# Clustered attention and two MoE layers on one core: another order of the kernel's first steps, and other engines for the first mask rows

## The chip, the cores and the metric

The kernel runs on one core of a Trainium2 chip. The core has five engines that run their own instruction streams and meet at semaphores: TensorE (PE in the profile, its weight loads PEld), VectorE (DVE), ScalarE (ACT), GpSimd (POOL) and SyncE (SP, which here only issues DMAs). The metric is device time in microseconds (us) of one execution, the median of several.

## The reference

There are 2 batches, 8 heads, 768 tokens, head size 64 and 16 centroids per head. What the change touches is the assignment and the mask:

```python
c_n = centroids / (np.linalg.norm(centroids, axis=-1, keepdims=True) + 1e-06)
q_assign = np.argmax(np.einsum('bhsd,hcd->bhsc', q_n, c_n), axis=-1)
k_assign = np.argmax(np.einsum('bhsd,hcd->bhsc', k_n, c_n), axis=-1)
mask = q_assign[:, :, :, None] == k_assign[:, :, None, :]
scores = scale * np.matmul(q, k.transpose(0, 1, 3, 2))
scores = np.where(mask, scores, -1000000000.0)
...
attn = attn / (np.sum(attn, axis=-1, keepdims=True) + 1e-09)
return np.matmul(attn, v).astype(np.float32)
```

A token attends only to tokens of its own cluster. The result goes through two feed-forward layers (`_moe_ref`, `_moe2_ref`), in fp32, which the change leaves as they are.

## The kernel before

All of it is one function, `tile_kernel`, whose order is the order in which it is written: each engine gets its instructions in that order and the semaphores are put in by the framework. Two reads of one PSUM tile by different engines are also put in order by a semaphore.

Attention goes over 8 pairs of heads (`pairs`) and for each over 12 steps (`order`: half of the queries, block of 128 queries, head of the pair). A step `n` is: `scores` (four matmuls into `s_ps`, of which there are two buffers: the products of the rounded `q1` and `k1` first, L382, then of `q2` and `k2`, L386), `maximum` (DVE, L395), `exponentials` (ACT, L403, into `p`), transposes of `p` (L439), and later the product with the values (L446). The mask is part of the scores: rows 64 to 80 of `q2` and `k2` hold a one-hot code of the cluster, times 2**60 on the query side, less 2**60, so that a pair of other clusters gets -2**60. For the first pair 32 rows are written, and these are what the change calls mask rows.

Before step 0 there is a head of the program, some 13 us long, in which little runs side by side:

1. `cn` (the centroids, 32 KB) is loaded; their norms come from ACT (L240 to L242) and DVE (L243 to L248); DVE scales `cn` (L249).
2. TensorE turns `cn` (L252, 64 rows out). DVE copies the even heads' half into rows 0 to 63 of `ct`, and then ACT the odd heads' half into rows 64 to 127 (`ct_copy`, L255); the rest of `ct` is zeros (L224).
3. `sims` (L309) multiplies `ct` with the raw queries `sq` and keys `sk` of the first pair, 384 KB each.
4. DVE alone finds the largest of each 16, breaks ties and makes the one-hot codes: L321, L335, L340, L346, L349, then per head L352 and the turning into rows L520 (`t3`, in PSUM).
5. Six instructions write the mask rows out of `t3` before step 0 and 1 can end, and a seventh and eighth follow for the second half of the queries: `q_rows` (L524, ACT) and plain copies of the key rows (L532, ACT for head `h0`, DVE for head `h1`).

Beside these, ACT makes `q1` and `k1` of both heads (L476 to L487), POOL the remainders (L481 to L497), DVE one (L499). `keep_warm` puts transposes of the identity on TensorE that nobody reads: 15 at the start, 3 after the turning of `cn`, 27 after `sims`, 18 and 9 around step 0 (all L215); the first waits for POOL to make the identity (`ident`). SP issues every DMA in order; the second pair's `sk` and `sq` are loaded once the first pair's are read.

Of the kernel before, what the change touches and what calls it, by code (L numbers as in the profile page):

```python
# [17 lines left out]
MASKED = float(2**60)  # L18

@with_exitstack  # L20
def tile_kernel(ctx, tc, q_t, k_t, q_s, k_s, v_l, cent, w_in, w_out, a_co, b_co, w_gate, w_val, w_o2, out):
    nc = tc.nc
    B, H, D, S = q_t.shape
    D //= 2
    NC = cent.shape[0] // H
    P = 128
# [12 lines left out]
    def r32(ap):  # L39
        return ap.bitcast(F32)  # L40

    nc.scalar.preload_act_table_set("natural_log_exp_and_others")
    ctx.enter_context(tc.manual_schedule())
    small = ctx.enter_context(tc.tile_pool(name="small", bufs=1, side="left"))
    r0_p = ctx.enter_context(tc.tile_pool(name="r0_p", bufs=1, side="left", reuse_waits="tile"))
# [135 lines left out]
            nc.sync.dma_start(out=t[key], in_=src[b, h])  # L181


    def load_pair(b, hp, keys=("sq", "sk")):
        for key in keys:
            live[key] = xs_p.tile([P, S], F32, tag=key, name=key)
            nc.sync.dma_start(out=live[key], in_=(q_s if key == "sq" else k_s)[b, hp])
# [6 lines left out]
    cn = as_p.tile([P, J, NC], F32, tag="t1", name="cn").rearrange("p j c -> p (j c)")[:, 0:D]  # L194
    nc.sync.dma_start(out=cn, in_=cent)
    load_pair(0, 0)
    for e in range(2):
        heads[0, e] = {}
    cst = small.tile([P, 24], F32, name="cst")
# [3 lines left out]
    xk1 = x_tile("xk")  # L203
    nc.sync.dma_start(out=xk1[0:D, :], in_=k_t[0, 1, 0:D, :])

    ident = base.tile([P, P], F32, name="ident")
    make_identity(nc, ident)

    def t_tile(name):
        return ps_t.tile([P, HB, P], F32, tag="t", name=name)  # L210

    def keep_warm(n, to, x=None):
        for _ in range(n):
            for j in range(HB):
                nc.tensor.transpose(to[:, j, :], ident if x is None else x[:, 0:P], ident)  # L215

    warm = ps_s.tile([P, S], F32, tag="s", name="w_ps")[:, 0:HALF].rearrange("p (j c) -> p j c", c=P)
    keep_warm(5, warm)

    wt_i = const.tile([P, NC], mybir.dt.int32, name="wt_i")  # L220
    nc.gpsimd.iota(wt_i, pattern=[[-1, NC]], base=NC, channel_multiplier=0)
    wt = const.tile([P, NC], F32, name="wt")
    ct = const.tile([P, H // 2, 2, NC], F32, name="ct")
    nc.vector.memset(ct, 0.0)  # L224
# [27 lines left out]
    nc.tensor.transpose(ct_ps, cn, ident)  # L252

    def ct_copy(copy, e):
        copy(  # L255
            out=ct[e * D:(e + 1) * D, :, e, :], in_=ct_ps.rearrange("p (h e c) -> p h e c", e=2, c=NC)[:, :, e, :]
        )
# [265 lines left out]
    def q_rows(t, half):
        nc.scalar.activation(  # L524
            out=t["q2"][D:D + 32, cols[half]], in_=t["t3"][32 * half:32 * half + 32, :],
            func=AF.Identity, scale=MASKED, bias=msk[32 * half:32 * half + 32, 1:2],
        )
# [950 lines left out]
```

## Time and profile before

| | |
|---|---|
| median of 3 runs | 771.9 us (771.74 to 772.0) |
| profiled execution | 771.61 us, of which the span of the trace is 769.8 us |
| PE busy | 763.1 us, 99% of the span |
| DVE, ACT, POOL busy | 78%, 65%, 59% |
| chain that ended last | PE 93%, ACT 3%, DVE 2% |

The span runs from the first instruction in the trace to the last; 1.8 us of the execution lie around it. A busy PE is one with a matmul on its way, and fillers count as busy. The chain is followed back from the last instruction, at each step to what released it.

### The profile page before, as it was taken

Reading aid. Unit: us, or ns where it says so; the run is one execution under the profiler, and the core shown is the slowest. Engines: PE = TensorE matmul, PEld = TensorE weight load, DVE = VectorE, ACT = ScalarE, POOL = GpSimd, SP = SyncE. Lnnn points to the kernel's source line nnn. Section 1 sums busy time; section 2 is a strip of 40 time slices with the busy share of each in tenths; the row PEclk is TensorE's granted clock in tenths of the full one; section 3 lists DMA queues with packets and bytes.
Section 4 is the critical chain, followed back from the end, with each engine's and each line's share of the span. In section 5 each row is a group of like instructions: output and inputs, shape, how many; then the busy total and the mean of one; then the engine's idle time right before and its main releaser. Section 6 shows DMA issues by size and latency. Waiting matters only on the chain.

```text
span 769.8 us, 11591 instructions
## 1 busy us (share of the span) xinstructions
PE 763.1 (99%) x4119; PEld 638.9 (83%) x4119; DVE 599.3 (78%) x919; ACT 504.1 (65%) x959; POOL 454.0 (59%) x429
## 2 busy tenths in 40 slices
PE   8999999999999999999999999999999999999998
PEld 7767677777768888888888888999999999999997
DVE  7888878788769999889999989996576665675454
ACT  7677768777867888687777678556554545444331
POOL 6667687667316676657777688674263554444310
PEclk9999999999999999999999999999999999999999
DMA  6456545453222211121111111023212212120013
GB/s 217 119 181 215 186 131 166 163 168 94 73 77 82 82 56 61 49 83 55 56 54 55 55 55 56 1 63 129 83 55 83 70 42 80 55 82 28 1 42 123
DMA packets 27209, 67.94 MB, mean 88 GB/s; under 512 B 4464, under 2 KB 10832, under 8 KB 27152
## 3 DMA queue, kind: packets, MB, share of 16 engines
q1 hardware_dynamic: 27152, 67.21, 26.8%
q8 instruction: 32, 0.52, 0.3%
q14 instruction: 25, 0.20, 0.1%
HBM read 59.48 MB, written 3.19 MB: 81 GB/s over the span
## 4 chain that ended last, share of the span: by engine, by line
PE 93%; ACT 3%; DVE 2%; POOL 1%; issue 1%; POOLq 0%; ACTq 0%; DVEq 0%
PE c_ps L1068 23%; PE acc L804 15%; PE h_ps L748 14%; PE acc L1125 13%; PE o_ps L446 8%; PE t_ps L439 7%; PE s_ps L382 4%; PE s_ps L386 4%; PE w_ps L215 1%; PE sim L309 1%; POOL tmp L765 1%; DVE st L395 1%; ACT p L403 1%; ACT tmp L773 0%; ACT tmp L763 0%
## 5 line engine op out<-in xcount | busy, mean ns | idle before, releaser
L1068 PE MATMUL c_ps<-r,wb 128*128 128x384 f32 x648 | 125.3, 336 | 0.0
L1068 PEld LDWEIGHTS c_ps<-r,wb 128*128 128x128 f32 x648 | 115.4, 188 | 6.0
L395 DVE TENSOR_REDUCE st<-s_ps 128x1 f32<-128x768 f32 x96 | 91.8, 956 | 31.8 <-PE s_ps L386 31.7
L765 POOL TENSOR_TENSOR tmp<-tmp 128x512 f32<-128x512 f32 x46 | 68.0, 1479 | 47.5 <-ACT tmp L764 47.1
L403 ACT ACTIVATE p<-s_ps,st 128x768 f32<-128x768 f32 x96 | 87.3, 909 | 7.6 <-DVE st L395 5.1
L1076 ACT COPY tmp<-c_ps 128x384 f32<-128x384 f32 x60 | 28.9, 481 | 86.9 <-PE c_ps L1068 86.9
L1147 POOL TENSOR_TENSOR part<-tmp,part 128x512 f32<-128x512 f32 x18 | 23.4, 1298 | 101.2 <-ACT tmp L1146 101.2
L439 PE MATMUL t_ps<-ident,p 128*128 128x128 f32 x576 | 76.5, 273 | 1.0 <-DVE pt L440 0.9
L439 PEld LDWEIGHTS t_ps<-ident,p 128*128 128x128 f32 x576 | 66.0, 140 | 5.6 <-DVE pt L440 1.2
L804 PE MATMUL acc<-g,r 128*128 128x512 f32 x288 | 69.1, 389 | 0.2 <-ACT part L811 0.2
L788 POOL TENSOR_TENSOR g<-td,tmp 128x512 fp32r<-128x512 f32 x45 | 58.5, 1300 | 18.0 <-DVE td L783 18.0
L1079 DVE TENSOR_TENSOR tmp<-tmp,c_ps 128x384 f32<-128x384 f32 x40 | 22.2, 554 | 58.9 <-ACT tmp L1076 45.1
L446 PE MATMUL o_ps<-pt,v 128*64 128x384 f32 x384 | 65.7, 491 | 0.1
L1068 PE MATMUL c_ps<-r,xw 128*128 128x384 f32 x336 | 65.4, 337 | 0.0
L440 ACT COPY pt<-t_ps 128x384 f32<-128x384 f32 x128 | 56.0, 481 | 14.1 <-PE t_ps L439 14.1
L804 PEld LDWEIGHTS acc<-g,r 128*128 128x128 f32 x288 | 54.0, 188 | 11.8 <-ACT part L811 0.7
L1068 PEld LDWEIGHTS c_ps<-r,xw 128*128 128x128 f32 x336 | 60.0, 188 | 3.7
L748 PE MATMUL h_ps<-r 128*128 128x512 f32 x252 | 60.5, 390 | 0.0
L1125 PE MATMUL acc<-wb,g 128*128 128x512 f32 x216 | 59.4, 394 | 0.0
L382 PE MATMUL s_ps<-k,q 128*128 128x512 f32 x192 | 57.7, 382 | 0.3 <-ACT p L403 0.2
L748 PEld LDWEIGHTS h_ps<-r 128*128 128x128 f32 x252 | 47.1, 188 | 10.4 <-issue 0.6
L446 PEld LDWEIGHTS o_ps<-pt,v 128*64 128x64 f32 x384 | 26.0, 137 | 35.1 <-issue 32.6
(169 smaller groups left out, 1789.6 us busy)
## 6 DMA issues: line engine op xcount, KB each, us to landing
raw<-w_in_dram SPq DMA_DIRECT2D x16, 512.0 KB
raw<-w_out_dram SPq DMA_DIRECT2D x16, 512.0 KB
raw<-w_val_dram SPq DMA_DIRECT2D x12, 512.0 KB
raw<-w_gate_dram SPq DMA_DIRECT2D x12, 512.0 KB
raw<-w_o_dram SPq DMA_DIRECT2D x12, 512.0 KB
xa<-q_t_dram SPq DMA_DIRECT2D x14, 384.0 KB
xa<-k_t_dram SPq DMA_DIRECT2D x14, 384.0 KB
sq<-q_s_dram SPq DMA_DIRECT2D x8, 384.0 KB
```

Of the source, the lines that this page charges most:

```text
L382: nc.tensor.matmul(s_ps[:, lo:hi], t["q1"][:, qs], t["k1"][:, lo:hi], start=True, stop=False)
L395: nc.vector.tensor_reduce(out=st[:, 0, k:k + 1], in_=live["s", b, hp, half, i, e], axis=AX.X, op=ALU.max, negate=True)
L403: nc.scalar.activation(out=p, in_=live.pop(("s", b, hp, half, i, e)), func=AF.Exp, bias=st[:, 0, k:k + 1], accum_out=st[:, 1, k:k + 1],)
L439: nc.tensor.transpose(t_ps[:, j, :], p[:, kb * P:(kb + 1) * P], ident)
L440: copy(out=pt[:, g * HB:(g + 1) * HB, i * P:(i + 1) * P], in_=t_ps)
L446: nc.tensor.matmul(live["o", b, hp, half][e * D:(e + 1) * D, :], heads[b, 2 * hp + e]["v"][:, kb, :], live["pt", b, hp, half, e][:, kb, :] ...
L748: nc.tensor.matmul(h_ps, w[:, wi, cs], x[:, xi, cc, :], start=(n == 0), stop=(n == 3 * NCC - 1))
L765: spread.tensor_tensor(out=tq, in0=tq, in1=tr, op=ALU.add)
L788: eng.tensor_tensor(out=g[:, 1, :], in0=td, in1=tr, op=ALU.mult)
L804: nc.tensor.matmul(acc[c], w[:, wi, cs], g[:, gi, :], start=(first and m == 0), stop=(last and m == 2))
L1068: nc.tensor.matmul(live2[key], set_of[f][:, wi, a, cs], x[xi][:, kc, :], start=(first and n == 0), stop=(n == last), skip_group_check=True,)
L1125: nc.tensor.matmul(acc2[j, c], g[:, gi, c * P:(c + 1) * P], w[:, wi, :], start=(f % 2 == 0 and m == 0), stop=(f % 2 == 1 and m == 2),)
```

## The change

The table load of ACT comes after an issue of `sk` on ACT's own DMA queue. TensorE gets two matmuls of zeros ahead of its first transposes. `cn` is copied into two blocks `cn2`, one times the parity of the head and one times its opposite (`par`, from a new `iota`), both are scaled and turned at once (128 rows out), and one DVE copy fills `ct`. The mask rows go to other engines, and one copy of ACT (`k1`, upper half, of `h1`) stands behind the first two of them. The second pair's `sq` is loaded ahead of its `sk`.

```diff
-    nc.scalar.preload_act_table_set("natural_log_exp_and_others")
...
-    load_pair(0, 0)
+    load_pair(0, 0, queues=(nc.sync, nc.scalar))
+    nc.scalar.preload_act_table_set("natural_log_exp_and_others")
...
+    oh = [rb_p.tile([P, HALF], F32, tag="rb", name="oh") for e in range(2)]
+    zero = oh[0][:, 0:P]
+    nc.vector.memset(zero, 0.0)
...
+    for j in range(HB - 1):
+        nc.tensor.matmul(warm[:, j, :], zero, zero, start=True, stop=True)
     keep_warm(5, warm)
...
+    nc.vector.tensor_tensor(
+        out=cn2.rearrange("p (e d) -> p e d", e=2), in0=cn.rearrange("p (o d) -> p o d", o=1).to_broadcast([P, 2, D]),
+        in1=par.to_broadcast([P, 2, D]), op=ALU.mult,
+    )
...
-    nc.vector.tensor_scalar_mul(out=cn, in0=cn, scalar1=ss[:, 3:4])
...
-    ct_ps = t_tile("ct_ps")[0:D, 0, :]
-    nc.tensor.transpose(ct_ps, cn, ident)
...
-    ct_copy(nc.vector.tensor_copy, 0)
+    nc.vector.tensor_scalar_mul(out=cn2, in0=cn2, scalar1=ss[:, 3:4])
+
+    ct_ps = t_tile("ct_ps")[:, 0, :]
+    nc.tensor.transpose(ct_ps, cn2, ident)
+    nc.vector.tensor_copy(out=ct.rearrange("p h e c -> p (h e c)"), in_=ct_ps)
...
-    ct_copy(nc.scalar.copy, 1)
...
-        nc.scalar.copy(out=t["k1"][D:P, :], in_=xk)
+        if e == 0:
+            nc.scalar.copy(out=t["k1"][D:P, :], in_=xk)
...
-    load_pair(*pairs[1], keys=("sk", "sq"))
+    load_pair(*pairs[1])
...
     q_rows(h0, 0)
-    for half, c in enumerate(cols):
-        for t, copy in ((h0, nc.scalar.copy), (h1, nc.vector.tensor_copy)):
-            copy(out=t["k2"][D:D + 32, c], in_=t["t3"][64 + 32 * half:96 + 32 * half, :])
+    k_rows(h0, 0, nc.scalar.copy)
+    nc.scalar.copy(out=h1["k1"][D:P, :], in_=xk1_up)
+    k_rows(h0, 1, nc.vector.tensor_copy)
+    q_rows(h1, 0)
+    k_rows(h1, 0, nc.vector.tensor_copy)
+    k_rows(h1, 1, nc.scalar.copy)
...
-    q_rows(h0, 1)
-    q_rows(h1, 0)
...
         if n == 1:
+            q_rows(h0, 1, on_dve=True)
             keep_warm(3, fill)
```

How the instructions then stand, at three places. First TensorE at the start of the program, before (`w_ps` is what fillers write, `ct_ps` the turned centroids):

```order
L215 MATMUL w_ps_135<-ident_130 128x128 [waits Pool_49]
L215 MATMUL w_ps_135<-ident_130 128x128 x14
L252 MATMUL ct_ps_180<-ident_130,cn_120 64x128 [waits DVE_49]
L215 MATMUL w_ps_135<-ident_130 128x128 x3
L309 MATMUL sim_196<-sq_122,ct_154 32x384 [waits DMAHW1_49,Activation_49]
L309 MATMUL sim_196<-sq_122,ct_154 32x384
```

and now, with two matmuls of zeros (read from `oh`) in front, and `sims` waiting for DVE instead of ACT:

```order
L223 MATMUL w_ps_138<-oh_130 128x128 [waits DVE_49]
L223 MATMUL w_ps_138<-oh_130 128x128
L219 MATMUL w_ps_138<-ident_133 128x128 [waits Pool_49]
L219 MATMUL w_ps_138<-ident_133 128x128 x14
L267 MATMUL ct_ps_188<-ident_133,cn_119 128x128 [waits DVE_49]
L219 MATMUL w_ps_138<-ident_133 128x128 x3
L318 MATMUL sim_203<-sq_121,ct_159 32x384 [waits DMAHW2_49,DVE_49]
```

The 15 transposes are still there, behind the zeros and ahead of the turning of the centroids.

Second ACT between `k1` and the first exponentials, before (`t3_262` and `q2_184`, `k2_186` are of `h0`; `t3_265`, `q2_188` of `h1`):

```order
L487 CAST k1_189<-sk_124 64x768
L524 ACTIVATE q2_184<-t3_262,msk_156 32x384 [waits DVE_49]
L532 CAST k2_186<-t3_262 32x384 x2
L524 ACTIVATE q2_184<-t3_262,msk_156 32x384
L524 ACTIVATE q2_188<-t3_265,msk_156 32x384 [waits DVE_49]
L403 ACTIVATE p_301,st_298<-s_ps_275,st_298 128x768 [waits DVE_49]
```

and now (`t3_268`, `q2_192`, `k2_194` of `h0`; `t3_271`, `q2_196`, `k2_198` of `h1`):

```order
L495 CAST k1_197<-sk_123 64x768
L541 ACTIVATE q2_192<-t3_268,msk_163 32x384 [waits DVE_49]
L544 CAST k2_194<-t3_268 32x384
L548 CAST k1_197<-sk_123 64x768
L541 ACTIVATE q2_196<-t3_271,msk_163 32x384 [waits DVE_49]
L544 CAST k2_198<-t3_271 32x384 [waits DVE_49]
L412 ACTIVATE p_307,st_304<-s_ps_281,st_304 128x768 [waits DVE_49]
```

The 64x768 copy (L548) has moved between the rows of `h0` and those of `h1`, and the last key rows now wait for DVE.

Third DVE at the same place, before:

```order
L520 STREAM_TRANSPOSE t3_262<-oh_165 128x384 [waits DVE_49,Activation_49]
L352 TENSOR_TENSOR oh_166<-wt_153,mx_259 128x12x16
L520 STREAM_TRANSPOSE t3_265<-oh_166 128x384 [waits DVE_49]
L532 CAST k2_190<-t3_265 32x384 [waits DVE_49]
L532 CAST k2_190<-t3_265 32x384
L389 MEMSET st_298 128x6
L395 TENSOR_REDUCE st_298<-s_ps_275 128x1 [waits PE_49]
```

and now:

```order
L530 STREAM_TRANSPOSE t3_268<-oh_130 128x384 [waits DVE_49]
L361 TENSOR_TENSOR oh_131<-wt_158,mx_265 128x12x16
L530 STREAM_TRANSPOSE t3_271<-oh_131 128x384 [waits DVE_49]
L544 CAST k2_194<-t3_268 32x384 [waits Activation_49]
L544 CAST k2_198<-t3_271 32x384 [waits Activation_49]
L398 MEMSET st_304 128x6
L404 TENSOR_REDUCE st_304<-s_ps_281 128x1 [waits PE_49]
L404 TENSOR_REDUCE st_304<-s_ps_315 128x1 [waits PE_49]
L537 TENSOR_SCALAR q2_192<-t3_268,msk_163 32x384
```

Both key-row copies of DVE now wait for ACT: by the values of the semaphore the first (`k2_194`) for ACT's copy of `h0`'s other key rows, the second (`k2_198`) for ACT's `q2_196` from the same `t3_271`. ACT's `k2_198` waits for DVE's.

## Rows read from the trace of the kernel before

**Rows 1.** PE in a stretch: us, busy (instructions), granted clock, DMA share, GB/s

```profile
40.00:700.00 660.00, 659.53 (x3528) 1.00 0.27 88
```

**Rows 2.** The chain that ended last, in order of time: start, us, what

```profile
5.68 1.17 PE sim L309 x8
...
13.84 0.60 PE s_ps L386 x2
...
14.46 0.97 DVE st L395
...
15.46 1.00 ACT p L403 x2
...
16.50 0.62 PE s_ps L382 x2
...
18.13 0.78 PE sim L309 x8
```

**Rows 3.** Timeline, 0 to 7 us: start, us, instruction, count, idle before and releaser

```profile
0.73 1.28 ACT L42 ACT_TABLE_LOAD   x1 [0.73 <-PEq L1469]
...
0.74 0.39 SPq L195 DMA_DIRECT2D cn<-cent_dram  x1
0.83 0.17 DVE L224 MEMSET ct<- 128x128 f32 x1 [0.83 <-PEq L1469]
...
1.18 0.42 SPq L187 DMA_DIRECT2D sq<-q_s_dram  x1
...
1.36 3.46 PE L215 MATMUL w_ps<-ident 128*128 128x128 f32 x15 [1.36 <-POOL ident masks.py:199]
...
2.51 0.26 ACT L240 ACTIVATE sq<-cn 128x64 f32<-128x64 f32 x1 [0.50 <-DMA cn<-cent_dram]
...
4.28 0.84 ACT L476 ACTIVATE q<-sq 64x768 fp32r<-64x768 f32 x1 [0.86 <-DMA sq<-q_s_dram]
4.29 0.26 DVE L249 TENSOR_SCALAR cn<-cn,cst 128x64 f32<-128x64 f32 x1
...
4.62 0.42 PE L252 MATMUL ct_ps<-ident,cn 128*64 128x128 f32 x1
...
5.08 0.22 DVE L255 COPY ct<-ct_ps 64x64 f32<-64x64 f32 x1 [0.52 <-PE ct_ps L252]
...
5.32 0.95 DVE L499 SCALAR_TENSOR_TENSOR q<-sq,q 64x768 fp32r<-64x768 f32 x1
...
5.61 0.82 PE L309 MATMUL sim<-sq,ct 128*32 128x384 f32 x2
...
6.77 3.17 PE L215 MATMUL w_ps<-ident 128*128 128x128 f32 x27
6.89 0.60 DVE L321 STREAM_TRANSPOSE t<-sim 128x384 f32<-128x384 f32 x1 [0.62 <-PE sim L309]
```

**Rows 4.** Timeline of ACT and DVE, 9 to 17.6 us

```profile
9.72 0.83 ACT L487 CAST k<-sk 64x768 fp32r<-64x768 f32 x1
...
9.92 0.35 DVE L352 TENSOR_TENSOR oh<-wt,mx 128x192 f32<-128x192 f32 x1
...
10.38 0.59 DVE L520 STREAM_TRANSPOSE t<-oh 128x384 f32<-128x384 f32 x1
...
11.01 0.57 ACT L524 ACTIVATE q<-t,msk 32x384 fp32r<-32x384 f32 x1 [0.45 <-DVE t L520]
...
11.59 0.95 ACT L532 CAST k<-t 32x384 fp32r<-32x384 f32 x2
...
11.88 1.13 DVE L532 CAST k<-t 32x384 fp32r<-32x384 f32 x2
...
12.57 1.17 ACT L524 ACTIVATE q<-t,msk 32x384 fp32r<-32x384 f32 x2
...
13.26 0.96 DVE L395 TENSOR_REDUCE st<-s_ps 128x1 f32<-128x768 f32 x1
...
16.30 0.96 DVE L395 TENSOR_REDUCE st<-s_ps 128x1 f32<-128x768 f32 x1 [0.88 <-PE s_ps L386]
```

More of the change, by code (lines that the diff above doesn't have):

```diff
@@ L181, in load_qk, with load_pair @@
             nc.sync.dma_start(out=t[key], in_=src[b, h])
-    def load_pair(b, hp, keys=("sq", "sk")):
-        for key in keys:
+    def load_pair(b, hp, keys=("sq", "sk"), queues=(nc.sync, nc.sync)):
+        for key, queue in zip(keys, queues):
             live[key] = xs_p.tile([P, S], F32, tag=key, name=key)
-            nc.sync.dma_start(out=live[key], in_=(q_s if key == "sq" else k_s)[b, hp])
+            queue.dma_start(out=live[key], in_=(q_s if key == "sq" else k_s)[b, hp])
     def load_v(b, h):
@@ L192, in load_v @@
         nc.sync.dma_start(out=t["v"], in_=v_l[b, h])
-    cn = as_p.tile([P, J, NC], F32, tag="t1", name="cn").rearrange("p j c -> p (j c)")[:, 0:D]
+    cn_t = as_p.tile([P, J, NC], F32, tag="t1", name="cn").rearrange("p j c -> p (j c)")
+    cn, cn2 = cn_t[:, 0:D], cn_t[:, D:3 * D]
     nc.sync.dma_start(out=cn, in_=cent)
-    load_pair(0, 0)
+    load_pair(0, 0, queues=(nc.sync, nc.scalar))
+    nc.scalar.preload_act_table_set("natural_log_exp_and_others")
     for e in range(2):
@@ L223, in tile_kernel @@
     ct = const.tile([P, H // 2, 2, NC], F32, name="ct")
-    nc.vector.memset(ct, 0.0)
+    par_i = const.tile([P, 2], mybir.dt.int32, name="par_i")
+    nc.gpsimd.iota(par_i, pattern=[[NC, 2]], base=NC, channel_multiplier=1)
+    par = const.tile([P, 2, 1], F32, name="par")
     msk = const.tile([P, 2], F32, name="msk")
@@ L230, in tile_kernel @@
         nc.vector.memset(msk[r, 1:2], -MASKED if g < 2 else 0.0)
-    oh = [rb_p.tile([P, HALF], F32, tag="rb", name="oh") for e in range(2)]
-    for e in range(2):
-        nc.vector.memset(oh[e], 0.0)
+    nc.vector.memset(oh[0][:, P:HALF], 0.0)
+    nc.vector.memset(oh[1], 0.0)
     nc.vector.tensor_copy(out=wt, in_=wt_i)
+    nc.vector.tensor_scalar(
+        out=par_i, in0=par_i, scalar1=NC.bit_length() - 1, scalar2=1, op0=ALU.logical_shift_right, op1=ALU.bitwise_and
+    )
+    nc.vector.tensor_copy(out=par.rearrange("p e o -> p (e o)"), in_=par_i)
     sq = as_p.tile([P, J, NC], F32, tag="sm", name="sq").rearrange("p j c -> p (j c)")[:, 0:D]
@@ L242, in tile_kernel @@
     nc.scalar.activation(out=ss[:, 1:2], in_=ss[:, 1:2], func=AF.Exp, scale=0.5)
+    nc.vector.tensor_tensor(
+        out=cn2.rearrange("p (e d) -> p e d", e=2), in0=cn.rearrange("p (o d) -> p o d", o=1).to_broadcast([P, 2, D]),
+        in1=par.to_broadcast([P, 2, D]), op=ALU.mult,
+    )
     nc.vector.reciprocal(out=ss[:, 2:3], in_=ss[:, 1:2])
@@ L248, in tile_kernel @@
     nc.vector.reciprocal(out=ss[:, 3:4], in_=ss[:, 2:3])
-    nc.vector.tensor_scalar_mul(out=cn, in0=cn, scalar1=ss[:, 3:4])
-    ct_ps = t_tile("ct_ps")[0:D, 0, :]
-    nc.tensor.transpose(ct_ps, cn, ident)
[L254 to L257, printed above, removed]
-    ct_copy(nc.vector.tensor_copy, 0)
+    nc.vector.tensor_scalar_mul(out=cn2, in0=cn2, scalar1=ss[:, 3:4])
+    ct_ps = t_tile("ct_ps")[:, 0, :]
+    nc.tensor.transpose(ct_ps, cn2, ident)
+    nc.vector.tensor_copy(out=ct.rearrange("p h e c -> p (h e c)"), in_=ct_ps)
     babs = cst[:, 6:11]
@@ L474, in tile_kernel @@
     xs = (live["sq"], live["sk"])
+    xk1_up = live["sk"][D:P, :]
     up = slice(D, P)
     nc.scalar.activation(out=h0["q1"][0:D, :], in_=xs[0][0:D, :], func=AF.Copy, scale=scale)
-    ct_copy(nc.scalar.copy, 1)
     keep_warm(1, warm)
@@ L521, in tile_kernel, with q_rows, k_rows @@
     del live["t1"], live["mx"], live["sm"]
[L523 to L527, printed above, removed]
-    q_rows(h0, 0)
-    for half, c in enumerate(cols):
-        for t, copy in ((h0, nc.scalar.copy), (h1, nc.vector.tensor_copy)):
-            copy(out=t["k2"][D:D + 32, c], in_=t["t3"][64 + 32 * half:96 + 32 * half, :])
+    def q_rows(t, half, on_dve=False):
+        g = slice(32 * half, 32 * half + 32)
+        out, rows = t["q2"][D:D + 32, cols[half]], t["t3"][g, :]
+        if on_dve:
+            nc.vector.tensor_scalar(
+                out=out, in0=rows, scalar1=MASKED, scalar2=msk[g, 1:2], op0=ALU.mult, op1=ALU.add
+            )
+        else:
+            nc.scalar.activation(out=out, in_=rows, func=AF.Identity, scale=MASKED, bias=msk[g, 1:2])
+    def k_rows(t, half, copy):
+        copy(out=t["k2"][D:D + 32, cols[half]], in_=t["t3"][64 + 32 * half:96 + 32 * half, :])
+    q_rows(h0, 0)
+    k_rows(h0, 0, nc.scalar.copy)
[4 more added lines that the diff above has]
+    k_rows(h1, 1, nc.scalar.copy)
     fill = ps_v.tile([P, HALF], F32, tag="o", name="w_ps").rearrange("p (j c) -> p j c", c=P)
-    q_rows(h0, 1)
-    q_rows(h1, 0)
     early = (20, 26, 38, 50, 62, 74, 80, 86, 92)
```

## The prediction

> **What bounds the kernel now.** I read the stretches of PE first: from 40 to 700 us TensorE is idle for 0.47 us in all, at a granted clock of 1.00 [rows 1]. Nothing in the body waits for anything else, so a change of the head can only move the whole body earlier or later, and the body has no idle time that could take up a late start. Then the chain in order of time: from step 0 on it goes from matmul to maximum to exponential to the matmul that needs the buffer back [rows 2], with gaps of some hundredths. So what counts is when the maxima of steps 0 and 1 start, 13.26 and 14.46 us now [rows 2, 4]: what they are late, the end is late. Last I read the timelines backwards from there. The maxima hang on the mask rows, those on `t3` (10.38 + 0.59 = 10.97 us [rows 4]), `t3` on a chain of DVE alone that starts at 6.89 us when `sims` is done, and `sims` on the copy of the turned centroids [rows 3].
>
> I work in two parts: the shift of DVE's start at 6.89, and the mask rows measured from `t3`.
>
> **The zeros and the clock.** [...] Leaving out the drain of the last transpose (0.42 us long, like L252), one follows the other after (3.46 - 0.42)/14 = 0.217 us.
>
> At this rate the 15 fill TensorE until 1.36 + 15 x 0.217 = 4.62 us, which is where the turning of the centroids starts; DVE had `cn` ready at 4.29 + 0.26 = 4.55 [rows 3]. So the queue of fillers ends just in time, and any work put ahead of it goes onto the path. The zeros start after a 128x128 memset as at 0.83 + 0.17 = 1.00 us [rows 3], about 1.05. An fp32 matmul that is not a transpose shows as two records (`sims` is four matmuls and 8 records [rows 2]), so two 128-column matmuls are 4 records of 0.217 = 0.87 us, and the transposes begin at 1.92 instead of 1.36: 0.56 us later. If they were one record each it would be 1.48, 0.12 us later; I take 0.56, as `sims` is the nearest row. The turning then starts at 5.18.
>
> **One copy instead of two.** From the start of the turning to `sims` it is 5.61 - 4.62 = 0.99 us now. With one copy: 0.42 for the turning, 0.04 to DVE, a 128x128 copy, 0.06 to PE. The copy is bounded by 0.22 (64 columns) and 0.59 (L520, 384 columns) [rows 3, 4]; 64 columns more, a fifth of the way, give 0.29. That is 0.81; but the turning and three fillers behind it take 4 x 0.217 = 0.87, so 0.87 holds and 0.12 us is saved. `sims` starts at 5.18 + 0.87 = 6.05, 0.44 late. The product by parity lies in DVE's wait for ACT between 2.5 and 3.5 us and costs nothing; were that cover gone, it would cost about the 0.35 of L352 [rows 4]. The scaling of 128 instead of 64 columns adds some 0.07 to 4.55, hidden by the queue of fillers.
>
> **`sims` itself.** Started 0.44 later it runs mostly or wholly after the rise of the clock, so it saves between 0 (rise as much later) and 1.17 - 0.78 = 0.39 us. I take 0.30, since the rise comes at the latest during `sims` now and TensorE starts 0.31 us earlier. DVE's start shifts by 0.44 - 0.30 = +0.14; bounds: +0.44, and with the zeros at one record each and the full 0.39, -0.39.
>
> **Keys on ACT's queue.** Nothing waits for `sk` now, so its earlier start gains nothing by itself. ACT's issue (0.39 to 0.43 as SP's) pushes its table load to end at 0.73 + 0.42 + 1.28 = 2.43, just before the centroids land at 2.51 [rows 3]: hidden with 0.08 to spare. What can cost is that `cn` now shares the DMA engines with 384 KB of keys. If `cn` lands d late, the turning waits only for d above 5.18 - 4.67 = 0.51, as fillers hold TensorE that long. Bounds for d: 0, and landing when the keys do. `sq`, as large, took from 1.18 to 4.28, 3.10 us, `cn` from 0.74 to 2.51, 1.77 [rows 3]: d is at most 1.33. I take d under 0.5, as `cn` is a twelfth of the keys, and keep 1.33 - 0.51 = +0.82 for the range. [...] No row of this trace has two queues loading at once.
>
> `sq` shares as well. Late by up to 0.6 us, ACT's L476 and then DVE's L499 would end at 4.28 + 0.6 + 0.84 + 0.04 + 0.95 = 6.71 [rows 3], still before 7.03 when DVE is to start: hidden.
>
> **One wait less.** L520 now also waits for ACT's old copy and starts 0.11 us after L352 ends (9.92 + 0.35 to 10.38 [rows 4]), where DVE's neighbours stand 0.03 to 0.04 apart. That semaphore goes: -0.07.
>
> **The mask rows.** Counted from `t3` = 10.97. Now: ACT's rows of `h0` end at 12.54, its last for `h1` at 12.57 + 1.17 = 13.74, and step 1's matmul starts at 13.84 [rows 2, 4]. After: ACT writes `q2` of `h0` (0.57) and half its key rows (0.48) until 12.06; then comes the moved 0.83 us copy, until 12.89; then `q2` of `h1` (0.58) until 13.47. DVE's copy for `h0` waits for ACT's and ends at about 12.67, near the 12.54 of now; its copy for `h1` waits for 13.47 and ends at 13.51 + 0.57 = 14.08. In line behind it on DVE stands the maximum of step 0: after the memset it starts at about 14.11 instead of 13.26, +0.85. ACT's last key rows wait for DVE: 14.12 to 14.60, step 1's matmul starts at 14.68 instead of 13.84, +0.84. I take +0.84; bounds 0.80 and 0.90 by the rounding of six durations. The copy's old place was free: ACT ended L487 at 10.55 and was idle for 0.45 [rows 4], and that idle time is not on the path. `q_rows(h0, 1)` on DVE lies in the 0.88 us of idle before the maximum of step 2 [rows 4] and costs nothing; without that cover 0.57. The second pair's `sk` is issued after the moved copy, some 1.2 us later than the last of the two now, and is needed only at `sims` of 18.1 us plus the shift.
>
> **Sum.** +0.14 - 0.07 + 0.84 = +0.91 us. On the profiled execution's 771.61 that is 772.5; that execution lies 0.3 below the median of the runs, so on the median 772.8. That is 0.12%; about 0.2%, 1.5 us, is what a measurement of this kernel tells from no change.
>
> **The rivals.**
>
> The clock rises early. [...] In this trace 27 transposes in a row keep 117 ns [rows 3], so they hold it at least. Worked out from rows: if real matmuls at 1.05 us raise the clock before the fillers are through, these are done by about 4 us, the turning starts at 4.67, takes 0.27, the copy 0.29, `sims` runs from 5.35 for 0.85, and DVE could start at 6.25. It then waits for L499, which ends at 6.11 to 6.71 by when `sq` lands, so it starts at 6.25 to 6.75, 0.14 to 0.64 before 6.89. The sum is then +0.13 to +0.63, 772.0 to 772.5. For it: TensorE starts earlier. Against: the rise now came 4 to 5 us after the first transposes, and 0.31 us is little of that.
>
> The centroids land late. Place: `cn` on SP's queue beside `sk` on ACT's. Up to d = 0.51 it costs nothing; each tenth above costs a tenth; from d = 0.51 + 0.63 = 1.14 on it is slower by 0.2%. At the bound of 1.33 the time is 771.9 + 0.91 + 0.82 = 773.6. For it: both issues fall at 0.73 us, and the whole head hangs on `cn`. Against: 32 KB is little, and the fillers cover 0.51.
>
> The waits at the mask rows do not reach the end. If the shift of step 0 were taken up further down, +0.07 is left, 772.0. Against: the 0.47 us of idle in 660 us.
>
> **The numbers.** Forecast, +0.3 to +1.3 us (772.2 to 773.2): 0.55. Early clock, 772.0 to 772.5: 0.17. Late centroids, 773.2 to 773.7: 0.17, of which half lie beyond 1.5 us. Shift taken up, 772.0: 0.05. What I have not seen, 0.06, in halves on either side. Slower by over 0.2%: 0.09 + 0.03 = 0.12; faster: 0.03; within: 0.85. The range leaves one in ten out on each side: 771.9 to 773.7.
>
> **What would show it.** In the trace of the changed kernel: the transposes starting near 1.9 us and the turning near 5.2; `sims` at 6.0 and of some 0.9 us; ACT's first activation at 2.5 if `cn` is on time; from the end of `t3` to the maximum of step 0 3.1 us instead of 2.3, with DVE's wait for ACT before its second key-row copy. The prediction is wrong if the span changes by more than the shift of step 1's maximum, or if that shift is not there.

## The result, and the profile after

The changed kernel takes 775.45 us (median of 6 runs, 775.08 to 776.84) against 771.72 us before (6 runs, 771.29 to 772.0): ratio 1.0052, 95% interval 1.0041 to 1.0062. It is slower by 3.7 us, where 0.9 us had been predicted, and above the predicted range of 771.9 to 773.7 us. The profiled execution is one of 775.42 us, with a span of 773.6 us, 3.8 us longer than before.

The head first, as in [rows 3]: the timeline of the changed kernel, 0 to 8 us.

```profile
1.05 1.22 PE L223 MATMUL w_ps<-oh 128*128 128x128 f32 x4 [1.05 <-DVE oh L209]
...
2.07 3.41 PE L219 MATMUL w_ps<-ident 128*128 128x128 f32 x15
...
3.71 0.26 ACT L251 ACTIVATE sq<-cn 128x64 f32<-128x64 f32 x1 [1.27 <-DMA cn<-cent_dram]
...
4.91 0.84 ACT L486 ACTIVATE q<-sq 64x768 fp32r<-64x768 f32 x1 [0.29 <-DMA sq<-q_s_dram]
...
5.83 0.33 PE L267 MATMUL ct_ps<-ident,cn 128*128 128x128 f32 x1 [0.36 <-DVE cn L264]
...
6.20 0.29 DVE L268 COPY ct<-ct_ps 128x128 f32<-128x128 f32 x1 [0.42 <-PE ct_ps L267]
...
6.55 0.52 PE L318 MATMUL sim<-sq,ct 128*32 128x384 f32 x2
...
7.49 0.60 DVE L330 STREAM_TRANSPOSE t<-sim 128x384 f32<-128x384 f32 x1
```

The zeros are four records and the copy takes 0.29 us, as worked out. But `cn` lands at 3.71 instead of 2.51 us (ACT's first read of it), and the turning waits for DVE's `cn`, no longer for the fillers. DVE starts at 7.49 instead of 6.89: +0.60.

Then the mask rows, as in [rows 4]: the same timeline, 10.8 to 16 us.

```profile
10.90 0.59 DVE L530 STREAM_TRANSPOSE t<-oh 128x384 f32<-128x384 f32 x1
...
11.53 0.57 ACT L541 ACTIVATE q<-t,msk 32x384 fp32r<-32x384 f32 x1 [1.44 <-DVE t L530]
...
12.12 0.47 ACT L544 CAST k<-t 32x384 fp32r<-32x384 f32 x1
12.61 0.83 ACT L548 CAST k<-sk 64x768 fp32r<-64x768 f32 x1
12.62 0.56 DVE L544 CAST k<-t 32x384 fp32r<-32x384 f32 x1 [0.25 <-ACT k L544]
...
13.46 0.57 ACT L541 ACTIVATE q<-t,msk 32x384 fp32r<-32x384 f32 x1
14.07 0.56 DVE L544 CAST k<-t 32x384 fp32r<-32x384 f32 x1 [0.89 <-ACT q L541]
14.66 0.47 ACT L544 CAST k<-t 32x384 fp32r<-32x384 f32 x1 [0.62 <-DVE k L544]
...
14.79 2.03 DVE L404 TENSOR_REDUCE st<-s_ps 128x1 f32<-128x768 f32 x2
```

`t3` is there at 11.49 (before 10.97, +0.52). DVE's second key-row copy waits 0.89 us for ACT, and step 0's maximum starts 3.30 us after `t3` instead of 2.29. Step 1's maximum starts at 15.86 (below) instead of 14.46 [rows 2], +1.40 = 0.52 + 0.88.

So far the sum holds but for `cn`. The rest came further down, as two later steps of the chain of waits show (start, us, what), after and before:

```profile
15.86 0.97 DVE st L404
...
29.62 1.33 PE sim L318 x8
30.95 5.11 PE o_ps L455 x24
```

```profile
27.53 0.78 PE sim L309 x8
28.31 4.02 PE o_ps L446 x24
```

The same matmuls start 2.09 us late, and take 1.64 us longer (1.33 + 5.11 against 0.78 + 4.02). The stretches of PE (us, busy and instructions of PE, PEld, DVE, ACT and POOL, granted clock, DMA share, GB/s) tell why, after and before:

```profile
25.00:30.00 5.00, 3.44 (x21) 2.11 (x23) 4.97 (x9) 2.95 (x9) 3.41 (x5) 0.97 0.37 126
30.00:40.00 10.00, 10.00 (x61) 5.68 (x54) 6.40 (x12) 4.76 (x11) 1.77 (x3) 0.84 0.19 45
40.00:700.00 660.00, 659.42 (x3536) 549.18 (x3535) 533.78 (x792) 453.96 (x859) 415.15 (x386) 1.00 0.27 88
```

```profile
25.00:30.00 5.00, 4.00 (x28) 1.94 (x29) 4.94 (x10) 4.48 (x10) 3.38 (x5) 1.00 0.14 54
30.00:40.00 10.00, 10.00 (x74) 7.96 (x70) 7.92 (x14) 6.34 (x16) 4.62 (x6) 1.00 0.32 86
```

After, PE is idle for 1.56 us between 25 and 30 us (before 1.00), and between 30 and 40 us it is busy throughout, at a granted clock of 0.84 (0.50 from 30 to 32 us, 0.72 from 32 to 34). From 40 us on [rows 1] nothing has changed. What makes PE wait at step 7 is seen in the timeline of DVE, POOL and PE, 22 to 28.1 us, before and after:

```profile
22.40 2.74 POOL L288 TENSOR_TENSOR q<-xa,q 64x256 fp32r<-64x256 f32 x3
...
22.97 0.57 DVE L340 TENSOR_TENSOR sm<-t,mx 128x384 f32<-128x384 f32 x1
23.58 0.97 DVE L346 TENSOR_TENSOR sm<-sm,wt 128x384 f32<-128x384 f32 x1
...
25.94 0.55 PE L439 MATMUL t_ps<-ident,p 128*128 128x128 f32 x3 [0.92 <-DVE pt L440]
```

```profile
23.00 2.13 POOL L297 TENSOR_TENSOR q<-xa,q 64x256 fp32r<-64x256 f32 x3
...
24.48 1.06 DVE L349 TENSOR_TENSOR sm<-t,mx 128x384 f32<-128x384 f32 x1
25.21 1.02 POOL L305 TENSOR_SCALAR k<-xa 128x768 fp32r<-128x768 f32 x1
25.57 1.06 DVE L355 TENSOR_TENSOR sm<-sm,wt 128x384 f32<-128x384 f32 x1
...
28.03 0.55 PE L448 MATMUL t_ps<-ident,p 128*128 128x128 f32 x3 [1.49 <-DVE pt L449]
```

These are work for the second pair: DVE compares the products with their largest (L340, now L349) and weighs the result (L346, now L355), ahead of step 6's maximum; POOL makes remainders in three passes (L288, now L297). What DVE's two take when POOL does nothing beside them is seen in the run e10 (below):

```profile
28.04 0.55 DVE L340 TENSOR_TENSOR sm<-t,mx 128x384 f32<-128x384 f32 x1
28.62 0.56 DVE L346 TENSOR_TENSOR sm<-sm,wt 128x384 f32<-128x384 f32 x1
```

Before, DVE came 0.57 us after POOL's first pass began, its comparison took 0.57 us, and it was mostly POOL that became longer (2.74 us); only the weighing paid (0.97). Now DVE comes 1.48 us after it, 0.1 us after the third pass began (23.00 + 2.13 - 0.74 = 24.39), and POOL takes 2.13 while both of DVE's instructions take 1.06: 0.58 us more than before in the two. DVE moved by 1.4 us, but POOL by 0.60 only: its work hangs on `sims` and `k1`, not on the mask rows.

The account: 1.39 (start of step 3's scores and of DVE behind it) + 0.70 (up to step 6's maximum, 0.58 of it in the two instructions) + 1.64 (matmuls at the lower clock) = 3.73 us, of the span's 3.8.

### The profile page after: what moved, and what is told of

It is laid out like the page before. It is cut to its first block, busy times and chain, and to the rows that moved or that the text cites. A ratio compares the mean times of both kernels' runs of the same rounds, so it can differ in the third digit from the quotient of the medians.

```text
span 773.6 us, 11601 instructions
## 1 busy us (share of the span) xinstructions
PE 765.5 (99%) x4123; PEld 639.8 (83%) x4123; DVE 601.1 (78%) x923; ACT 503.1 (65%) x957; POOL 453.5 (59%) x430
## 4 chain that ended last, share of the span: by engine, by line
PE 91%; ACT 3%; DVE 2%; POOL 2%; issue 1%; DMA 0%; SPq 0%; POOLq 0%; ACTq 0%; DVEq 0%
PE c_ps L1087 23%; PE acc L823 15%; PE h_ps L767 14%; PE acc L1144 13%; PE o_ps L455 8%; PE t_ps L448 7%; PE s_ps L391 4%; PE s_ps L395 4%; POOL tmp L784 1%; PE sim L318 1%; ACT p L412 1%; DVE st L404 1%; DMA sq<-q_s_dram 0%; ACT tmp L792 0%; ACT tmp L782 0%
```

## The experiments

Lines are those of the changed kernel, or of the kernel before where that is the base. Each was timed beside the kernel before (771.2 to 771.7 us in these). What is told of an early or late start comes from this table: the start of an instruction of DVE less that of the same one before (us), in the profiled executions. Only what changes along a row is sure: DVE's start after `sims` varies by 0.6 us between profiles of the same head (see "The zeros and one copy" below), which shifts a whole row.

| kernel | maximum of step 1 | step 6 | step 9 | step 15 | at 205 us | at 760 us |
|---|---|---|---|---|---|---|
| changed | 1.39 | 2.09 | 3.73 | 3.73 | 3.84 | 3.83 |
| e1_keys_back | 0.81 | 1.48 | 3.12 | 3.12 | 3.01 | 3.28 |
| e2_copy_back | 1.05 | 1.16 | 1.16 | 2.06 | 2.20 | 2.19 |
| e3_mask_back | 0.96 | 1.07 | 1.08 | 2.04 | 1.96 | 1.94 |
| e4_fill_hole | 1.80 | 2.48 | 2.48 | 2.46 | 2.63 | 2.62 |
| e5_before_keys_act | 1.84 | 1.96 | 1.95 | 2.22 | 2.19 | 2.18 |
| e6_zeros_parity | -0.52 | -0.44 | -0.44 | 0.27 | 0.42 | 0.42 |
| e7_zeros_parity_12 | -0.46 | -0.38 | -0.38 | -0.38 | -0.26 | -0.28 |
| e8_pool_later | 0.28 | 0.40 | 0.40 | 0.40 | 0.31 | 0.58 |
| e9_after_pool_later | 1.54 | 1.66 | 1.65 | 2.73 | 2.85 | 2.89 |
| e15_zeros_12_late_rows | -0.29 | -0.08 | -0.08 | 0.84 | 0.65 | 0.92 |
| e16_dve_read_2_no_tile | 0.27 | 0.33 | 0.33 | 0.33 | 0.26 | 0.25 |
| e17_dve_read_3_no_tile | 0.86 | 1.13 | 1.12 | 1.14 | 1.14 | 1.13 |
| e18_tile_alone | -0.13 | -0.09 | -0.09 | -0.10 | -0.16 | 3.72 |

**Parts taken back.** Three kernels undo one part each of the change: the keys' queue, the place of the 64x768 copy, and the mask rows with that copy.

```diff
# e1_keys_back
-    load_pair(0, 0, queues=(nc.sync, nc.scalar))
+    load_pair(0, 0)
# e2_copy_back: the copy is ACT's old one, ahead of the mask rows
-        if e == 0:
-            nc.scalar.copy(out=t["k1"][D:P, :], in_=xk)
+        nc.scalar.copy(out=t["k1"][D:P, :], in_=xk)
...
-    nc.scalar.copy(out=h1["k1"][D:P, :], in_=xk1_up)
# e3_mask_back: as e2, and the old loop over the mask rows, with q_rows(h0, 1) and q_rows(h1, 0) behind it
```

> The changed kernel with the first keys back on SP's queue and the table load first. Chain theory (the late start of step 1 is 0.5 us of late centroids and 0.9 us of mask rows; the rest of the 3.7 us is a longer run of DVE's in steps 4 to 7 and a fall of TensorE's clock in the hole that this leaves): the centroids land at 2.5 us, DVE's start after the similarities falls from 7.49 to about 7.0, step 1's maximum from 15.86 to about 15.4; 774.9 us if the hole and the fall stay, 772.6 if both go. Rival (keys on the second queue cost nothing that reaches the end): 775.4.

> The changed kernel with only the 64x768 copy of ACT back in its old place, ahead of the mask rows. Chain theory: the mask rows of the second head start 0.83 us sooner, from the turned one-hot codes to step 1's maximum it is about 3.6 us instead of 4.4; 774.6 us if the hole and the fall of the clock stay, 772.3 if they go. Rival (the waits between ACT and DVE cost it, not the copy): step 1's maximum stays within 0.3 us of 15.86, 775.3.

> The changed kernel with the mask rows and the copy as in the kernel before; zeros, parity blocks and the keys on ACT's queue stay. Chain theory: from the turned codes to step 1's maximum 3.5 us as before, step 1's maximum at about 15.0; 774.5 us if the hole and the fall stay, 772.3 if they go. Rival (late centroids alone bring the fall): 774.5 with the clock falling near 30 us again.

Measured: 774.37 us (1.0032, 1.0020 to 1.0043), 773.11 (1.0017, 1.0008 to 1.0026) and 772.85 (1.0016, 1.0007 to 1.0025). With the keys on SP's queue `cn` lands at 2.57 us again, and 1.1 us come back; DVE still meets POOL there (1.02 and 1.06 us), PE waits 1.47 us at step 7, and the clock falls (0.90 from 26 to 30 us). With the copy in its old place 2.3 us come back, more than the 0.88 that it delays, and with the mask rows 2.6. In the profiles of e2 and e3 `cn` was even later than in the changed kernel (4.23 and 4.15 us), but the comparison takes 0.55 and 0.69 us, PE waits 0.89 and 1.04 us at step 7, and the table shows no loss between steps 6 and 9. So the copy gives back more than it delays because with it the meeting of DVE and POOL goes too.

**Parts put in.** The kernel before with the keys' queue alone; and with the zeros, the parity and the one copy alone, with 15 transposes and with 12.

```diff
# e5_before_keys_act
-    load_pair(0, 0)
+    load_pair(0, 0, queues=(nc.sync, nc.scalar))
+    nc.scalar.preload_act_table_set("natural_log_exp_and_others")
# e6_zeros_parity: the changed kernel with the edits of e1 and e3; e7_zeros_parity_12, besides:
-    keep_warm(5, warm)
+    keep_warm(4, warm)
```

> The kernel before with one part of the change: the first keys on ACT's queue and the table load behind that issue. Late centroids: they land 1.1 to 1.7 us late, DVE's start after the similarities moves by about 1 us (nothing covers it here, since the fillers end at 4.62 us), and POOL moves with it, so that the rest of the body only shifts: 772.6 to 773.0 us. If a late head by itself brings the fall of the clock: 774.4. If the move costs nothing: 771.7.

> The changed kernel with the keys' queue and the mask rows as before; zeros, parity blocks, one copy and the order of the second pair's loads stay. By the trace of the run with the keys back, the fillers hold the turning of the centroids until 5.1 to 5.3 us and the single copy and the faster similarities give it back: the turned codes at 10.9 us as before, 771.6 us. If zeros and parity cost by themselves: above 772.2.

> As the run with zeros and parity alone, with 12 instead of 15 transposes behind the zeros. If the queue of fillers is what holds the turning, it starts at about 4.7 instead of 5.1 us and all that follows is 0.4 to 0.5 us sooner: 771.1 us. If not: as the other, 771.6.

Measured: 773.46 (1.0020, 1.0011 to 1.0029), 772.24 (1.0009, 1.0000 to 1.0018), 771.89 (1.0006, 0.9997 to 1.0015). The keys' queue alone costs 1.9 us: `cn` lands at 4.22 us, and DVE starts 1.27 us late. The steps start 1.84 us late, since PE runs out of fillers and waits for the turning, and the clock falls behind this wait, going by the fillers and by the mean clock of the profiled execution, 0.998. Timeline of PE in e5:

```profile
6.31 0.30 PE L252 MATMUL ct_ps<-ident,cn 128*64 128x128 f32 x1 [1.64 <-DVE cn L249]
...
8.01 4.71 PE L215 MATMUL w_ps<-ident 128*128 128x128 f32 x27
```

These 27 fillers took 3.17 us before [rows 3], and step 0's second products stand behind them.

e6 and e7 end 0.6 and 0.8 us above what was expected of them. In their profiles the steps start 0.5 us earlier, about as far as the start of an unchanged head varies, so that this is not shown to come from the zeros and the one copy. e7's profiled execution is the fastest of its 11 (771.30), and where the others lose isn't known. In the profile of e6 the 0.5 us are lost at 41 us (table, step 15). Timeline of SP's issues, DVE and PE there:

```profile
35.20 0.47 SPq L431 DMA_DIRECT2D rd<-rs  x1
...
37.43 1.12 SPq L438 DMA_DIRECT2D rb<-rd  x2
...
40.71 0.56 DVE L463 TENSOR_TENSOR x<-o_ps,rb 128x384 f32<-128x384 f32 x1 [0.62 <-DMA rb<-rd]
...
41.32 0.87 PE L455 MATMUL o_ps<-pt,v 128*64 128x384 f32 x4 [0.87 <-DVE x L463]
```

The reciprocals of the sums go through memory (`rd`, `rb`). The first load back waits for the store and is issued 2.23 us after it, where it is 1.37 after the changed kernel's store (36.96 and 38.33 us), and PE waits. The same shows in e2, e3, e9 and e15 (2.1 to 2.4 us; waits of 0.9 to 1.2), and not in the others. Why the load is sometimes released some 0.9 us later was not found.

**The meeting of DVE and POOL.** Three kernels leave DVE's work as it is and change what it meets: 12 transposes fill PE's wait at step 7; one pass more on POOL (0.83 us) moves POOL's work back, on top of e1 and of the changed kernel.

```diff
# e4_fill_hole
+            if n == 7 and j == 1:
+                keep_warm(4, fill)
# e8_pool_later (on e1_keys_back), e9_after_pool_later (on the changed kernel)
     k_rest(h1, xk1[0:D, :])
+    nc.gpsimd.tensor_scalar(out=xk1[0:D, :], in0=xk1[0:D, :], scalar1=1.0, scalar2=0.0, op0=ALU.mult, op1=ALU.add)
```

> The changed kernel with 12 more transposes that nobody reads, in TensorE's 1.5 us hole at step 7. Theory that the hole lets the clock fall: the granted clock is 1.00 throughout, and the 1.6 us that the slow matmuls after 29.7 us take more go: 773.8 us. Rival (the fall has another cause, or costs nothing that reaches the end): 775.4 or, with the transposes in the way, up to 775.8.

> The run with the keys back, with one more 64x768 pass of POOL (0.83 us, nobody reads it) ahead of POOL's work for the second pair, so that POOL is as late against the steps as the mask rows make DVE. If DVE's long operations of step 6 and TensorE's hole come from where POOL's passes fall against DVE's: the comparison at step 6 takes 0.57 us again instead of 1.02, the hole is 0.9 us, the clock does not fall, 772.5 us. If the hole and the fall belong to the late mask rows themselves: 774.4, the same as with the keys back.

> The changed kernel with one pass more on GpSimd (64x768, 0.83 us) ahead of its work for the second pair. Theory of the meeting of VectorE and GpSimd: the shift of step 1, +1.4 us, stays, while the comparisons of step 6 take 0.55 and 0.97 us instead of 1.06 each, TensorE's wait at step 7 is about 0.9 instead of 1.49 us and the clock doesn't fall; 773.0 to 773.4 us against 775.45. Rival, that late centroids and mask rows cost what they cost whatever GpSimd does: 775.4 or more.

Measured: 774.75 (1.0040, 1.0028 to 1.0053), 772.71 (1.0017, 1.0008 to 1.0026) and 774.10 (1.0032, 1.0020 to 1.0045). More work on POOL makes e1 1.7 us and the changed kernel 1.35 us faster. In e9 the rows of before are back:

```profile
24.04 2.75 POOL L297 TENSOR_TENSOR q<-xa,q 64x256 fp32r<-64x256 f32 x3
...
24.62 0.57 DVE L349 TENSOR_TENSOR sm<-t,mx 128x384 f32<-128x384 f32 x1
25.23 0.97 DVE L355 TENSOR_TENSOR sm<-sm,wt 128x384 f32<-128x384 f32 x1
...
27.60 0.55 PE L448 MATMUL t_ps<-ident,p 128*128 128x128 f32 x3 [0.91 <-DVE pt L449]
```

Again DVE comes 0.58 us after POOL's first pass, POOL pays, and the clock stays at 1.00. e9 misses its expectation of 773.0 to 773.4 by 0.7; its profiled execution (774.48) lost 1.08 us at `rb` (table, step 15), and whether the others did is not recorded. With PE's wait filled the mean clock is 0.999 or 1.000 in all runs of e4 (0.998 in four of six of the changed kernel) and steps 6 to 9 lose nothing, but the comparison and the weighing still take 1.02 and 1.06 us, and the median gains only 0.7 us, where 1.6 had been expected. Its head was 0.4 us later than the changed kernel's in the profile.

**DVE made late in the kernel before.** Does a late DVE do this without the change? Useless work on DVE ahead of step 0's maximum: two, three and five memsets of `oh`, then two and three maxima over it.

```diff
# e10, e11, e12: 2, 3, 5 times, on the kernel before
+        nc.vector.memset(oh[0], 0.0)
# e13, e14: 2, 3 times, into a new tile; e16, e17 the same into cst[:, 23:24]
+    spare = small.tile([P, 1], F32, name="spare")
+        nc.vector.tensor_reduce(out=spare, in_=oh[0], axis=mybir.AxisListType.X, op=ALU.max)
# e18: that tile and one memset of it
```

> The kernel before with two useless memsets (128x384, 0.39 us each) on VectorE behind its key-row copies, ahead of the maximum of step 0; nothing else is changed. Step 0's maximum starts 0.78 us late, step 1's about 0.55 (it had 0.24 of idle ahead of it). That the body only shifts as a whole: 772.2 us. Theory of the meeting: VectorE's comparisons of step 6 come 0.55 us nearer to GpSimd's passes, which stay where they are; 772.2 if they still get past, up to 774 if not.

> As the run with two memsets, with three: step 0's maximum 1.17 us late, step 1's about 0.95, which is near what the changed kernel's VectorE is late against GpSimd (1.40 against 0.63). That the body only shifts: 772.6 us. Theory of the meeting: comparisons of 1.06 us in step 6, a wait of about 1.5 us at step 7 and a fall of the clock behind it, 774 to 775 us, with none of the change's parts in it.

> As the run with two memsets, with five: step 0's maximum 1.95 us late, step 1's about 1.7. That the body only shifts: 773.4 us. Theory of the meeting: VectorE's comparisons of step 6 then fall between GpSimd's passes or into the next ones, which isn't known beforehand; if they fall between, the time is 773.4 or less than with three memsets in spite of two more; if not, about 775.5.

Measured: 775.95, 776.94 and 777.21 us (1.0055, 1.0067, 1.0073). These are misses: the 18 fillers ahead of step 0's second products read `oh` and waited for the memsets, 3.9 us in e10, and the clock fell there (0.57 from 12 to 20 us; the 18 fillers took 4.10 us, for 2.18 before), so that step 1 came 5 us late. They only show that DVE 5 us late meets no pass of POOL in step 6 (0.55 and 0.56 us).

> The kernel before with two useless maxima over a one-hot tile (128x384, about 0.56 us each) on VectorE behind its key-row copies; other engines only read that tile too, so nobody waits for them (in the runs with memsets TensorE's 18 fillers did). Step 0's maximum 1.15 us late, step 1's about 0.94. That the body only shifts as a whole: 772.5 us. Theory of the meeting: GpSimd stays where it was, VectorE's comparisons of step 6 take 1.06 us each beside it, TensorE waits some 1.5 us at step 7, the clock falls behind that in most runs: 774 to 775 us, with none of the change's parts in it.

> As the run with two useless maxima, with three: step 1 about 1.5 us late. That the body only shifts: 773.1 us. Theory of the meeting: the comparisons come half a microsecond later still against GpSimd's passes, whose next gap lies there; either 773 to 773.5 us if they hit it, or 775 if not. Which of the two isn't known beforehand.

Measured: 775.72 (1.0057, 1.0045 to 1.0070) and 777.97 (1.0081, 1.0067 to 1.0095). The first number is what the meeting would give, but the trace says otherwise: at 205 us e13 is 0.69 us late and e14 1.53, and 3.9 us more come in the feed-forward layers, where neither has an edit. So the tile was taken out, and tried alone.

> As the run with two useless maxima on VectorE, with their output in a free column of a tile that the kernel before has already, so that no tile lies elsewhere in the memory. VectorE is 0.8 us late in the steps and the comparisons stay at about 0.62 and 0.98 us as there: the shift alone, 772.1 to 772.7 us. If the delay of VectorE by itself were what cost 4.5 us in the run with the tile: 775.7 us again.

> The same with three: VectorE 1.3 us late, which is the changed kernel's 1.39, the comparisons of step 6 some 0.77 and 1.06 us and TensorE's wait at step 7 1.2 us as in the run with the tile: 773.2 us in executions in which the clock doesn't fall behind that wait, 774.4 in those in which it does.

> The kernel before with the tile of 4 bytes a partition alone, one memset of 0.06 us and no maxima. If the place of the tiles behind it is what made the feed-forward part 3.8 us longer in the two runs with useless maxima: 775.2 to 775.8 us. If not: 771.6 us.

Measured: 772.01 (1.0006, 0.9998 to 1.0015), 772.82 (1.0021, 1.0012 to 1.0030) and 774.98 (1.0047, 1.0034 to 1.0059). The tile of 4 bytes costs 3.4 us by itself, with its one memset of 0.06 us (774.98 against 771.53). Without it, DVE made late by two maxima is passed on as it is; made late by three it meets POOL half:

```profile
22.05 2.12 POOL L288 TENSOR_TENSOR q<-xa,q 64x256 fp32r<-64x256 f32 x3
...
23.84 0.74 DVE L340 TENSOR_TENSOR sm<-t,mx 128x384 f32<-128x384 f32 x1
...
24.61 1.06 DVE L346 TENSOR_TENSOR sm<-sm,wt 128x384 f32<-128x384 f32 x1
...
27.07 0.55 PE L439 MATMUL t_ps<-ident,p 128*128 128x128 f32 x3 [1.18 <-DVE pt L440]
```

The comparison here begins 1.79 us after POOL's first pass and 0.40 us after the third began (22.05 + 2.12 - 0.72 = 23.45), and the steps lose 0.27 us. Nine of the 11 runs of e17 lie at 772.7 to 773.2 us with a mean clock of 0.999 or 1.000, the other two at 774.2 with 0.998: going by the mean clock, a fall costs about 1.4 us. What decides is thus the place of DVE against POOL's passes: begun 0.5 to 1.2 us after the first (before, e2, e3, e5 to e9, e16) the comparison takes 0.55 to 0.69 us, at 1.48 to 1.51 (the change, e1, e4) 1.02 to 1.06, at 1.79 (e17) 0.74.

**A version to use.** The zeros with 12 transposes, and one piece of the mask rows: `q_rows(h0, 1)` on DVE behind step 1's maximum.

```diff
# e15_zeros_12_late_rows: as e7, and
-    q_rows(h0, 1)
...
+            q_rows(h0, 1, on_dve=True)
```

> Zeros, parity and one copy with 12 transposes at the start, as in the run with 12, keys and mask rows as before; and of the mask rows one piece of the change: the query rows of the second half of head h0 go to VectorE behind step 1's maximum. Step 1's matmul then waits for 0.57 us less of ScalarE, and its maximum directly follows step 0's: 0.2 us earlier against step 0. If such a shift reaches the end, 771.4 to 771.7 us; if VectorE's place beside GpSimd in step 6 decides instead, 772 us or more.

Measured: 772.35 (1.0016, 1.0007 to 1.0025). It misses the 771.4 to 771.7 us hoped for: its profile is early until step 9 and loses 0.92 us at `rb`, while the comparison takes 0.66 us, so that POOL isn't what decides here. Neither this nor e7 beats the kernel before.

## Why the prediction was wrong

**The step that failed** is in its first paragraph: "a change of the head can only move the whole body earlier or later". That rested on PE's 0.47 us of idle from 40 us on [rows 1], which is right and held: the table's columns from 205 us to the end agree in all kernels but those with the new tile and, by 0.3 us, e1, e8 and e15. It said nothing of steps 2 to 12, between 16 and 40 us. There PE waited 0.92 us for DVE at step 7 in the profile before already, and DVE and POOL share a stretch of work in step 6. The head doesn't move as a whole either: the mask rows move DVE and not POOL. That cost 0.70 us in step 6, and the wait of 1.49 us behind it was followed by 1.64 us for the clock. e8 and e9 show the first (POOL moved, both gone); in e4, where the wait is filled, the clock didn't fall; e17 shows that a late DVE alone brings a smaller form of it (0.27 us, and a lower mean clock in two of 11 runs). No rival had this. The prediction's own sign came: the span grew by 3.83 us, step 1's maximum moved by 1.40.

In the rows the comparison and the weighing take 0.55 and 0.56 us with no instruction of POOL beside them (e10), and 1.06 each behind an instruction of POOL that began earlier (in the changed kernel the weighing ends at 26.63, 0.40 after POOL's 25.21 + 1.02 = 26.23). Three passes of POOL that find DVE under way get longer instead (2.74 for 2.13), and DVE's maxima and copies, with one input, keep their 0.94 to 0.96 and 0.54 to 0.55 us beside POOL. What the two engines hinder each other by, no run shows.

**Late centroids** was a rival at 0.17. I took d under 0.5; it was 1.20 us in the profiled execution, and 0.97 to 1.72 in five others with the keys on ACT's queue (against 2.51), beyond my upper bound of 1.33 in three. With d = 1.20 the rival's own sum gives 0.91 + 0.69 = 1.60; the start of step 1 had 1.40. In DVE's +0.60 the turning is 1.21 late (5.83), from there to `sims` 0.27 is saved (6.55 - 5.83 = 0.72 for 0.99), and `sims` takes 0.39 less; 0.05 comes from L509 on DVE, which the prediction called hidden and which ends at 6.52 + 0.95 = 7.47. "32 KB is little" was no reason: `cn` and `sk` are issued together at 0.73 us, in the changed kernel both queues keep the 16 DMA engines busy in the first 8 us (37.8% and 14.4% of their time), and with the keys back on SP's queue `cn` is in time (2.57 us for 3.71). The prediction should have taken its upper bound.

**The zeros and one copy.** Four records, the copy's 0.29 us and the turning's start behind the fillers (5.27 us in e1, with the keys back, for 5.18) are as worked out. The +0.14 can't be told from no change: the start of DVE varies by 0.6 us over profiles of the same code up to there (6.42 to 7.05 us in nine kernels with the head of before, mean 6.71). With zeros and the keys on SP's queue it is 6.38 to 6.91 (e1, e6, e8), with them on ACT's 7.49 to 8.01 (the change, e2, e3, e4, e9). No run shows the 0.30 us that the sum took for `sims` behind the rise of the clock, whose moment differs between profiles (below); in the changed kernel `sims` took 0.39 less, the upper bound.

**One wait less**: `t3` +0.52 after +0.60, so -0.08 for -0.07. **The mask rows**: 0.88 for 0.84, within their bounds (step 0's maximum, counted from `t3`, 1.01 for 0.85). DVE's second copy waited for ACT as said, and the row on DVE (L537) was hidden.

**Early clock** did not come in the changed kernel, where all 15 transposes keep 0.42 us each (3.41 us in all). The moment of the first rise, told from durations, differs between profiles by more than the zeros could move it: the first transpose shorter than 0.40 us starts at 4.2 us in e6 and e8 and at 4.0 in e2 and e3, with zeros (the 15 take 2.94, 2.88, 2.86 and 2.78 us), but all up to 6.4 us keep 0.42 in e4, with zeros too (3.41, and 0.84 for the three fillers at 6.00 us); without them the first starts at 4.2 in e5 (3.31) and 4.4 in e11 (3.41), and all up to 5.3 us keep 0.42 in the kernel before (3.46, and 0.85 for the three at 4.83). So no run shows that zeros bring the rise forward, and the prediction took its moment from a single profile.

**What stays open.** Two of the six runs of the changed kernel show a mean clock of 1.000 and still take 775.5 us. Only the profiled execution has a trace, so the 1.64 us for the clock are shown for that one alone, and where these two lose as much isn't known; `rb` as in e9 would be about 1.1 of it, which is only argued.

## What to carry to other kernels

An engine that is busy all the time in the body proves that a shift is passed on there, not in the steps between; read each junction on the way, and above all which two engines work side by side and whether both move by the same amount. Work that delays one of two neighbours can cost more than its length (the copy of 0.83 us, put back, gave 2.3), and extra work on the other can pay (0.83 us more on POOL took 1.35 and 1.7 us off). A small load on which the whole head hangs should not be issued beside a big one from another queue: here it landed 0.97 to 1.72 us late in six profiles.

## What the runs showed of the hardware

A tile of 4 bytes a partition, never read, made matmuls of the feed-forward layers slower, where no edit stands. That the cause is the place of everything allocated behind it is argued, not shown (groups by line and form, 300 to 550 us: engine, operation, tiles, shapes, count, busy us, mean ns, idle before; before, then e18):

```profile
L804 PE MATMUL acc<-g,r 128*128 128x512 f32 x192 | 46.0, 389 | 0.0
...
L804 PE MATMUL acc<-g,wb 128*128 128x512 f32 x144 | 34.6, 389 | 0.0
```

```profile
L806 PE MATMUL acc<-g,r 128*128 128x512 f32 x192 | 47.2, 396 | 0.0
...
L806 PE MATMUL acc<-g,wb 128*128 128x512 f32 x144 | 35.6, 396 | 0.0
```

6 to 7 ns in 389 are 2.2 us in these two groups. Which address matters, if it is that, was not tried. The change's own small tiles (`par`, `par_i`) do not do this: its shift is 3.84 us at 205 and 3.83 at 760 us.

Second, PE's wait of 1.49 us at step 7 was followed by a fall of the granted clock (0.50 from 30 to 32 us), and so was that of 1.47 in e1 (0.90 from 26 to 30 us). Behind that of 1.64 at the turning in e5 the 27 fillers took 4.71 us for 3.17, at a mean clock of 0.998 for the whole execution, and in e10 to e12, with waits of 3.9 to 5.4, the clock was 0.57, 0.79 and 0.57 from 12 to 20 us. Waits at step 7 of 0.92 in the kernel before, 0.91 in e9 and 1.21 in e14 left it at 1.00 from 26 to 40 us; behind those of 0.89 to 1.04 in e2, e3, e5 to e8, e15, e16 and e18 and that of 1.18 in e17 the table shows no loss between steps 6 and 9. And transposes alone were enough for the first rise: in e5 PE had run nothing else when they became shorter at 4.2 us (3.31 us for the 15, for 3.46 before, and 0.30 for the turning, for 0.42). The page's clock column does not show the first rise (in the kernel before it is 1.00 from the start), but the durations do: two records of `sims` take 0.82 us at 5.61 us before, much as in the changed kernel at 30.06 us, where the granted clock is 0.50 (0.86), and 0.52 at 27.46 us before, where it is 1.00.
